# One fused attention and MLP kernel on one core: q loaded in 1 KB runs with token groups outermost, 64x64 state tiles, a new load order and a list-scheduled TensorE order

## The chip, the cores and the metric

The kernel runs on one core of one Trainium2 chip. The metric is device time in microseconds (us), from the start of the program to its end, so smaller is better. The kernel before takes 224.86 us (median of 3 runs, 224.59 to 225.25). Every later comparison ran both kernels in turn on one chip. On this core most executions of one kernel agree within about 1%; a run that is over 1.5% above the fastest of its kernel counts as slow and is left out of ratios. The medians quoted include every run; where a slow run is among them the text says so.

## The reference

Linear attention with decay over 4 batches, 8 heads, 768 tokens and head size 64, then an MLP with a "snake" activation on the 3072 tokens, 512 features and 2048 hidden features:

```python
# attention, block by block (per head, lam is the decay)
intra = einsum('bhic,bhjc->bhij', qb, kb) * Dmask          # lam ** (i - j), lower triangle
out   = einsum('bhij,bhjd->bhid', intra, vb) + einsum('bhid,bhde->bhie', qb * lam_pow, kv_state)
kv_state = lam_block * kv_state + einsum('bhsd,bhse->bhde', kb_dec, vb)
# MLP on x = (tokens, heads * 64)
h = x @ w_in
s = sin(alpha * h)
g = h + s * s / (alpha + 1e-9)
return g @ w_out                                           # (3072, 512) float32
```

## The kernel before

A step is 128 tokens of one batch, all 8 heads; there are 24 steps, and six in a row share one state. A chunk is four steps, 512 tokens, and the MLP works on chunks. The decay is folded into q and k ("scaling"): q is multiplied by lam to the power n, k by lam to the power -n, so that the mask is only triangular. Per step TensorE does:

- *transposes* of q and k (from step 13 on a DMA transposes them instead),
- *scores*, k·q, eight matmuls of 128 columns (`att_S`),
- *inter*, the state times q (`att_O`, first half), *intra*, v times the masked scores (second half),
- *state*, k times v, added to the state in PSUM.

Between the attention groups stand the *big matmuls*, 512 columns each: 64 a chunk for w_in (stage A, `grp_A`) and 64 a chunk for w_out (stage B, `grp_B`). A0 is stage A of chunk 0, and so on. After A0 and B0 come A1 with the attention of chunk 2, and then a steady state in which B of one chunk and A of the next alternate, with two chunks' worth of lead in the attention.

```python
def load_one(nme, s):                       # q, k and v alike: 256-byte runs (64 float32)
    ...
    a = src[b, :, n * BL:(n + 1) * BL, :].rearrange("h p d -> p h d")
    rec_load(lambda e: e.dma_start(dst[r][:, :, :], a), ...)

def prep(s, fast=False, soft=()):           # scaling of k and q, on GpSimd or on VectorE
    ...
    dve_k, dve_q = s == 3, fast and s != 2
    done = rec("DVE" if dve_k else "POOL", lambda e: e.tensor_tensor(k2[c], k32[r][:, :, :], Lk_b, ALU.mult), ...)
    rec("DVE" if dve_q else "POOL", lambda e: e.tensor_tensor(q2[c], q32[r][:, :, :], Lq_b, ALU.mult), ...)

def att_S(s):                               # scores
    for jp in range(HP):                    # head pairs
        for h in range(2):
            rows = slice(64 * h, 64 * h + 64)
            e.matmul(A_ps[:, 4 * h + jp, :], qkT[j][rows, 4 + jp, :], qkT[j][rows, jp, :])
    ...                                     # VectorE: S_m = A_ps * mask

def att_O(s, bank=None):
    if has_state:                           # inter: block-diagonal 128x128 state, four matmuls
        for jp in range(HP):
            e.matmul(dst[:, jp, :], Zs[(s - 1) % 2][:, jp, :], qkT[jq][:, jp, :], ...)
    for jp in range(HP):                    # intra
        for h in range(2):
            e.matmul(dst[64 * h:64 * h + 64, jp, :], v2[c][:, 2 * jp + h, :], S_m[j][:, 4 * h + jp, :], ...)
    ...
    rec("ACT", lambda e: e.copy(xT[x][:, :, col:col + 128], dst), ...)      # x copy
    ...                                     # then the state matmuls, and two copies of the state into Zs
```

A recorder collects these operations with their dependencies, and a scheduling function lays them out on the engines with assumed durations. For TensorE it keeps the order of the program; the other engines take whichever ready operation is first. In stage B0 the attention groups of steps 4 to 7 are placed by hand between the 16 w_out groups:

```python
T_B, S_B, O_B = (2, 6, 10, 12), (3, 7, 11, 13), (5, 10, 12, 15)
...
for m4 in range(4):
    for s4 in range(4):
        op = grp_B(0, s4, m4, banks[s4])
        i = 4 * m4 + s4
        if i in T_B: att_T(4 + T_B.index(i))
        if i in S_B: att_S(...); prep_next(...)
        if i in O_B: att_O(...); prep_v_next(...)
```

GpSimd squares most of the sines (`u`), scales most of q and k and issues the loads of the weights; ScalarE does the sines (`t`) and most copies out of PSUM; VectorE does the masks, the sums (`gT`), the squares that are left, and some of the scaling.

## Time and profile before

224.86 us; the profiled execution spans 222.9 us. Where each stage starts, by the first big matmul of it in the timeline:

| | A0 | B0 | A1 | B1 | end |
|---|---|---|---|---|---|
| start, us | 23.04 | 37.77 | 60.50 | 81.48 | 222.9 |
| length, us | 14.73 | 22.73 | 20.98 | 141.4 | |

The page cuts the span in 40 equal slices of 5.6 us; a digit is the busy share in tenths, for PEclk the clock granted to TensorE:

```profile
PE   6865999998999999999999999999999999999995
...
PEclk9999799999999999999999999999999999999999
DMA  6999999999999999999999533063031011100212
```

TensorE is busy all the time after the start. The DMA engines are busy up to slice 22. The clock is full but for slice 5, where the first big matmuls start.

The groups of the attention matmuls and of two ScalarE copies (line, engine, operation, tile, inputs, shapes, count, then busy us in all and mean ns of one, then idle time before them and its cause):

```profile
L448 PE MATMUL A_ps<-qkT 64*128 64x128 bf16 x192 | 9.5, 218 | 1.1 <-DVE qkT L439 1.0
L469 PE MATMUL A_ps<-qkT,Zs 128*128 128x128 bf16 x68 | 6.6, 219 | 0.2 <-DVE S_m L453 0.2
```

```profile
L496 ACT CAST Zs<-Z_ps 64x256 bf16<-64x256 f32 x40 | 14.6, 366 | 1.6 <-DVE qkT L439 1.0
L482 ACT CAST xT<-A_ps 128x512 bf16<-128x512 f32 x20 | 11.7, 586 | 15.1 <-PE A_ps L473 15.0
```

L448 is scores, L469 inter (four 128x128 matmuls), L482 the x copy, L496 the state copy, of which each step has two. Matmul ends overlap, so the time of a group is better read from starts. In the timeline of the steady state (start, us from first start to last end, engine, line and so on):

```profile
124.64 0.40 PE L448 MATMUL A_ps<-qkT 64*128 64x128 bf16 x8
124.97 1.04 PE L509 MATMUL m_ps<-xT,w 128*128 128x512 bf16 x4
...
128.44 0.39 PE L469 MATMUL A_ps<-qkT,Zs 128*128 128x128 bf16 x4
128.75 0.41 PE L473 MATMUL A_ps<-S_m,v_2 128*64 128x128 bf16 x8
```

Eight scores take 124.97 - 124.64 = 0.33 us, inter 128.75 - 128.44 = 0.31 us. From one scores group to the next it is 8.14 us in steady state (I call this the period), of which 32 big matmuls are 6.9.

The load queue, q1, with packets, megabytes and the time of its packets as a share of 16 engines' span:

```profile
q1 hardware_dynamic: 86640, 21.90, 52.3%
```

And one detail that mattered later: at the end of A0, VectorE and GpSimd, in their own timelines:

```profile
39.07 1.21 DVE L407 TENSOR_TENSOR qk_4<-q_4,Lq 128x512 bf16<-128x512 f32 x1
```

### The profile page before, as it was taken

The page shows a single profiled execution, that of the slowest core. Times are in us where ns is not written, and L with a number is a line of the kernel's source. Part 1 is how long each engine was busy: PE and PEld are TensorE (multiplying, and loading weights), DVE is VectorE, ACT ScalarE, POOL GpSimd, SP SyncE. Part 2 cuts the span into 40 slices and gives each one's busy share as a digit, 9 for nine tenths or more (in the row PEclk, how much of TensorE's full clock was granted, in tenths as well). Part 3 has the DMA queues.
Part 4 walks back from the last instruction along what each step waited for, and adds up shares of the span by engine and source line. Part 5 has one row for each costly group of instructions (what it writes and reads, how often), then busy time and mean ns, then how long its engine had stood idle before and what let it go on. Part 6 is the DMA issues. An engine that isn't in the chain of part 4 may idle for free.

```text
span 222.9 us, 3787 instructions
## 1 busy us (share of the span) xinstructions
PE 209.1 (94%) x1513; PEld 102.9 (46%) x1539; DVE 119.7 (54%) x160; ACT 121.8 (55%) x216; POOL 133.9 (60%) x141
## 2 busy tenths in 40 slices
PE   6865999998999999999999999999999999999995
PEld 2443344454555444445445444445445444444454
DVE  2674189736868994645545454553553535544300
ACT  3354688131498976575575556566556435544220
POOL 3464378661389998668768867867845553355000
PEclk9999799999999999999999999999999999999999
DMA  6999999999999999999999533063031011100212
GB/s 133 219 216 201 195 196 220 162 229 229 268 284 221 222 201 236 215 244 180 245 221 201 141 94 94 1 96 96 19 79 47 0 50 47 47 37 10 79 65 94
DMA packets 94513, 32.50 MB, mean 146 GB/s; under 512 B 87184, under 2 KB 91552, under 8 KB 94496
## 3 DMA queue, kind: packets, MB, share of 16 engines
q1 hardware_dynamic: 86640, 21.90, 52.3%
q0 software_dynamic: 4224, 4.19, 11.4%
q10 hardware_dynamic: 3632, 6.17, 7.6%
q8 instruction: 12, 0.20, 0.4%
q14 instruction: 5, 0.04, 0.1%
HBM read 27.28 MB, written 6.29 MB: 151 GB/s over the span
## 4 chain that ended last, share of the span: by engine, by line
PE 81%; DVE 6%; SPq 5%; DMA 3%; ACT 2%; issue 2%; POOL 0%
PE m_ps L509 34%; PE m_ps L537 34%; SPq L335 5%; PE A_ps L473 3%; PE A_ps L448 3%; DMA v_3<-in_v_dram 3%; DVE gT L527 2%; PE A_ps L469 2%; PE m_ps L562 2%; DVE S_m L453 1%; PE A_ps L434 1%; PE Z_ps L488 1%; PE A_ps L436 1%; DVE u_3 L525 1%; DVE qkT L439 1%
## 5 line engine op out<-in xcount | busy, mean ns | idle before, releaser
L509 PE MATMUL m_ps<-xT,w 128*128 128x512 bf16 x366 | 92.5, 382 | 2.3 <-issue 1.7
L537 PE MATMUL m_ps<-w,gT 128*128 128x512 bf16 x362 | 90.6, 379 | 0.6 <-issue 0.3
L537 PEld LDWEIGHTS m_ps<-w,gT 128*128 128x128 bf16 x368 | 34.9, 98 | 42.2 <-ACT osb L549 1.3
L509 PEld LDWEIGHTS m_ps<-xT,w 128*128 128x128 bf16 x384 | 35.1, 98 | 41.3 <-issue 1.5
L453 DVE TENSOR_TENSOR S_m<-A_ps,mask 128x1024 bf16<-128x1024 f32 x24 | 29.4, 1223 | 9.7 <-PE A_ps L448 9.7
L525 POOL TENSOR_TENSOR u_0<-t_0 128x512 bf16<-128x512 bf16 x16 | 16.6, 1038 | 13.9 <-ACT t_0 L513 13.9
L527 DVE SCALAR_TENSOR_TENSOR gT<-u_3,r_sb,m_ps 128x512 bf16<-128x512 bf16 x16 | 11.9, 744 | 15.0 <-POOL u_3 L525 14.9
L482 ACT CAST xT<-A_ps 128x512 bf16<-128x512 f32 x20 | 11.7, 586 | 15.1 <-PE A_ps L473 15.0
L525 POOL TENSOR_TENSOR u_2<-t_2 128x512 bf16<-128x512 bf16 x15 | 15.6, 1037 | 7.3 <-ACT t_2 L513 7.3
L525 POOL TENSOR_TENSOR u_4<-t_4 128x512 bf16<-128x512 bf16 x15 | 15.6, 1039 | 7.0 <-ACT t_4 L513 7.0
L527 DVE SCALAR_TENSOR_TENSOR gT<-u_5,r_sb,m_ps 128x512 bf16<-128x512 bf16 x16 | 11.9, 746 | 14.1 <-POOL u_5 L525 14.1
L527 DVE SCALAR_TENSOR_TENSOR gT<-u_1,r_sb,m_ps 128x512 bf16<-128x512 bf16 x16 | 11.9, 744 | 14.0 <-POOL u_1 L525 14.0
L527 DVE SCALAR_TENSOR_TENSOR gT<-u_0,r_sb,m_ps 128x512 bf16<-128x512 bf16 x16 | 11.9, 743 | 11.5 <-POOL u_0 L525 11.5
L549 ACT COPY osb<-m_ps 128x512 f32<-128x512 f32 x19 | 11.1, 585 | 11.7 <-PE m_ps L537 11.7
L525 POOL TENSOR_TENSOR u_5<-t_5 128x512 bf16<-128x512 bf16 x12 | 12.5, 1039 | 7.9 <-ACT t_5 L513 7.8
L513 ACT ACTIVATE t_0<-m_ps,alpha_sb 128x512 bf16<-128x512 f32 x16 | 11.0, 685 | 10.8 <-PE m_ps L509 10.8
L513 ACT ACTIVATE t_2<-m_ps,alpha_sb 128x512 bf16<-128x512 f32 x16 | 11.0, 687 | 10.7 <-PE m_ps L509 10.5
L525 POOL TENSOR_TENSOR u_3<-t_3 128x512 bf16<-128x512 bf16 x12 | 12.5, 1038 | 7.3 <-ACT t_3 L513 7.2
L513 ACT ACTIVATE t_4<-m_ps,alpha_sb 128x512 bf16<-128x512 f32 x16 | 11.0, 687 | 10.7 <-PE m_ps L509 10.7
L525 POOL TENSOR_TENSOR u_1<-t_1 128x512 bf16<-128x512 bf16 x12 | 12.4, 1037 | 7.2 <-ACT t_1 L513 7.2
L496 ACT CAST Zs<-Z_ps 64x256 bf16<-64x256 f32 x40 | 14.6, 366 | 1.6 <-DVE qkT L439 1.0
L513 ACT ACTIVATE t_3<-m_ps,alpha_sb 128x512 bf16<-128x512 f32 x16 | 11.0, 687 | 8.0 <-PE m_ps L509 8.0
(190 smaller groups left out, 238.0 us busy)
## 6 DMA issues: line engine op xcount, KB each, us to landing
out_dram<-osb ACTq DMA_DIRECT2D x23, 256.0 KB, 2.7
w<-in_moe_w_in_dram POOLq DMA_DIRECT2D x4, 512.0 KB, 11.5
w<-in_moe_w_out_dram POOLq DMA_DIRECT2D x4, 512.0 KB, 12.8
k_0<-in_k_dram SPq DMA_DIRECT2D x4, 256.0 KB, 5.1
q_0<-in_q_dram SPq DMA_DIRECT2D x4, 256.0 KB, 4.8
k_1<-in_k_dram SPq DMA_DIRECT2D x4, 256.0 KB, 5.2
q_1<-in_q_dram SPq DMA_DIRECT2D x4, 256.0 KB, 5.6
v_0<-in_v_dram SPq DMA_DIRECT2D x4, 256.0 KB, 4.9
```

The costliest lines, as they stand in the source:

```text
L335: rec_load(lambda e: e.dma_start(dst[r][:, :, :], a), [f"{nme}32.{r}"], f"{nme}{r}", 321000, [gate[s]] if s in gate else [])
L448: last = e.matmul(A_ps[:, 4 * h + jp, :], qkT[j][rows, 4 + jp, :], qkT[j][rows, jp, :])
L453: rec("DVE", lambda e: e.tensor_tensor(S_m[j2][:, :, :], A_ps[:, :, :], mask_b, ALU.mult), 1.25, reads=["S0", "S1", "mask"], writes=[f"S_m ...
L473: last = e.matmul(dst[64 * h:64 * h + 64, jp, :], v2[c][:, 2 * jp + h, :], S_m[j][:, 4 * h + jp, :], start=(not has_state and jp == 0), st ...
L482: rec("ACT", lambda e: e.copy(xT[x][:, :, col:col + 128], dst), 0.6, reads=[key], writes=[f"x.{x}.{s % 4}"], prio=-1)
L496: rec("ACT", lambda e, rows=rows, cols=cols: e.copy(Zs[j][rows, :, cols], Z_ps[rows, :, :]), 0.4, reads=["Z"], writes=[f"Zs.{j}"])
L509: last = e.matmul(m_ps[i][:, :], w1[:, kc, 128 * m:128 * (m + 1)], xT[x][:, kc, :], start=(kc == 0), stop=(kc == NKC - 1))
L513: rec("ACT", lambda e: e.activation(t16[tt][:, :], m_ps[i][:, :], ACTF.Sin, scale=alpha_sb[:, m:m + 1]), 0.65, reads=[f"m.{i}", "alpha"], ...
L525: return e.tensor_tensor(u16[tt][:, :], t16[tt][:, :], t16[tt][:, :], ALU.mult)
L527: rec("DVE", lambda e: e.scalar_tensor_tensor(out=gT[g][:, m, :], in0=u16[tt][:, :], scalar=r_sb[:, m:m + 1], in1=m_ps[i][:, :], op0=ALU.m ...
L537: last = e.matmul(m_ps[bank][:, :], gT[g][:, m, 128 * s4:128 * (s4 + 1)], w2[:, m, :], start=(m == 0), stop=(m == NM - 1))
L549: rec("ACT", lambda e: e.copy(osb[o][:, :], m_ps[bank][:, :]), 0.6, reads=[f"m.{bank}"], writes=[f"o.{o}"])
```

## The change

The intent was to shorten the start and the first B stage, and to take work off TensorE:

1. q comes in runs of four tokens, 1 KB. Partition p holds tokens 4i to 4i+3 of one head pair, with p = 4i + g: token groups outermost, head pairs g innermost. So the columns of the transposed q of one head pair lie 4 elements (8 bytes) apart, and attention's output comes out in the order (t, i). The x copy writes it back in token order, with a step of 8 bytes.
2. k and q of steps 0 to 3 are loaded first and v last; transposes, scores and masks of these steps are done before v is there.
3. The state is kept as eight 64x64 tiles, not as four block-diagonal 128x128 ones; one state copy instead of two. The state matmuls go before inter and intra.
4. TensorE's order is found by list scheduling in a window of 40 groups, with a slack of 0.2 us; the hand placement in B0 goes. Some work changes its engine and the loads of w_out are issued at other points.

The core of the diff (cuts marked):

```diff
@@ schedule
-                    op = pe_seq[pe_at]                 # TensorE in the order of the program
...
+                if e == "PE":
+                    ready = [o for o in ready if pe_rank[o] < pe_at + window]
...
+                op = min((o for o in ready if max(free[e], ready_at[o]) <= t0 + (slack if e == "PE" else 0) + 1e-9),
+                         key=lambda o: (o.prio, o.idx))
@@ load_one
+            if nme == "q":
+                for h in range(2):
+                    a = src[b, h::2, n * BL:(n + 1) * BL, :].rearrange("g (p t) d -> p g (t d)", t=4)
+                    rec_load(lambda e, h=h, a=a: e.dma_start(
+                        q32[r][:, h, :, :].rearrange("p t d -> p (t d)"), a), ...)
@@ attention
+        def q_cols(j, rows, jp):
+            return qkT[j][rows, 0:4, jp::4]
...
-                        last = e.matmul(A_ps[:, 4 * h + jp, :], qkT[j][rows, 4 + jp, :], qkT[j][rows, jp, :])
+                        last = e.matmul(A_ps[:, 4 * h + jp, :].rearrange("p (t i) -> p t i", t=4),
+                                        qkT[j][rows, 4 + jp, :], q_cols(j, rows, jp))
...
-                        e.matmul(dst[:, jp, :], Zs[(s - 1) % 2][:, jp, :], qkT[jq][:, jp, :],
-                                 start=(jp == 0), stop=False, skip_group_check=True)
+                        for h in range(2):
+                            rows = slice(64 * h, 64 * h + 64)
+                            e.matmul(dst[rows, jp, :].rearrange("p (t i) -> p t i", t=4), Zs[(s - 1) % 2][rows, jp, :],
+                                     q_cols(jq, rows, jp), start=(jp == 0), stop=False, skip_group_check=True)
...
-            rec("ACT", lambda e: e.copy(xT[x][:, :, col:col + 128], dst), 0.6, reads=[key],
+            copy(eng, xT[x][:, :, col:col + 128].rearrange("p a (i t) -> p a t i", t=4),
+                 dst.rearrange("p a (t i) -> p a t i", t=4), 0.75, reads=[key], writes=[f"x.{x}.{s % 4}"], prio=-1)
...
-                for h in range(2):
-                    rows, cols = slice(64 * h, 64 * h + 64), slice(64 * h, 64 * h + 64)
-                    rec("ACT", lambda e, rows=rows, cols=cols: e.copy(
-                        Zs[j][rows, :, cols], Z_ps[rows, :, :]), 0.4, reads=["Z"], writes=[f"Zs.{j}"])
+                rec("ACT", lambda e: e.copy(Zs[s % 2][:, :, :], Z_ps[:, :, :]), 0.4, reads=["Z"],
+                    writes=[f"Zs.{s % 2}"], prio=-2)
@@ program
-        for what in ("k0", "q0", "k1", "q1", "v0", "k2", "q2", "v1", "k3", "q3", "v2", "v3"):
+        for what in ("k0", "q0", "k1", "q1", "k2", "q2", "k3", "q3", "v0", "v1", "v2", "v3"):
...
+        w2_block(0, soft=[op])
...
         for m in range(NM):
             op = grp_A(0, m)
-            if m in W2_A:
-                w_block(6 + W2_A.index(m), after=[op])
-        prep_next(4, fast=True, soft=[op])
+            if m == 12:
+                w2_block(1, after=[op])
+        prep_next(4, soft=[op], eng_q="DVE")
...
+        att_T(4, bank=spare)
+        for s in range(4, 8):
+            prep(s + 1, soft=[op], eng_q="DVE" if s == 6 else "POOL")
+            prep_v_next(s + 1, [op])
+            att_S(s)
+            if s < 7:
+                att_T(s + 1, bank=spare)
+            att_O(s)
```

## The prediction

> **What bounds the kernel now.** TensorE is busy 209.1 of 222.9 us (busy table); 34% + 34% of the chain that ended last are the big matmuls. The windows show four stages:
> - 0 to 23.04 us: bound by loads. The DMA engines are saturated from 2.5 us; each 256 KB load lands 1.18 us after the last. The chain is SyncE issues, v_3 landing at 19.1, its cast, x and state copies, the last attention matmuls, the first big matmul at 23.04. The first w_in block arrives only then too (0.5 us wait). The clock has fallen: the first big matmuls are 0.43 us apart, later 0.216.
> - First B stage with attention 4 to 7, to 60.5: TensorE idle 1.8 of 22.7 us, on qkT, masks, q scaling, loads.
> - To 81.5: idle 0.5, GpSimd 93% busy.
> - To 206: no gaps. One attention step takes 8.14 us: 32 big matmuls (6.9), 1.2 of attention (scores 0.33 + 0.09 on entry, inter 0.31, intra 0.25, state 0.23). Only less TensorE work helps.
>
> **What the change does.**
> 1. q in 1 KB runs. The load queue's 86,640 packets, mostly 256 B, took 52.3% of 16 engines' span, 21.5 ns each; output packets (1.7 KB) 75 ns. The Trainium skill, "DMA: Bandwidth & Descriptors", Specifications, puts line rate at 512 B and more; the trace agrees (12 against 23 GB/s per engine). Estimate: a q load falls from 1.18 to 0.75 us, 1.7 us over four, on the chain.
> 2. k and q first, v last: transposes, scores, masks of steps 0 to 3 are done before v arrives; after v_3 remain cast, O and x copy (2.3 us, against 3.9 now). The first w_in half block competes with v_2 and v_3 and takes back about 1 us. Big matmuls start at 20.6; gain of 1 and 2 together 2.4 us.
> 3. List scheduling fills idle time in the B stage and after: 1.2 us.
> 4. 64x64 state tiles: eight small matmuls in pairs instead of four full ones. From the intra group's rate 0.31 falls to 0.23, less one more tile switch: 0.07 x 17 = 1.2 us.
> 5. One transposed step fewer on TensorE: 0.45 us.
> 6. Off the path: one state copy instead of two on ScalarE (0.76 to 0.4), strided x copies (0.59 to 0.75).
>
> Scores and inter now read q with a step of 8 bytes. The Trainium skill, "SBUF — State Buffer", Door 1, says that accesses hitting a 16-byte line twice keep full rate, which this does. No trace shows it yet; I assume no loss.
>
> Sum 5.3 us: predicted **219.5 us**, 8 in 10 between **216.8 and 222.0**. Faster by over 2% **0.62**, within 2% **0.35**, slower **0.03**.
>
> **What would show each step.** (1) The load queue falls to about 68,000 packets, its share by 6 to 8 points. (2) First big matmul at 20 to 21.2 us, v_3 landing near 18.3. (3) From the first B matmul to the second A stage 21.3 us instead of 22.7. (4) Steady period 8.05 to 8.10 us; inter 0.23. (5) Twelve qkT copies from PSUM, twelve DMA transposes.
>
> **What would make it wrong.** Strided q halving the matmul rate (+0.3 us per step, about +7 us). w_in delaying v_3, or late for chunk 0, so that the start gains nothing. A low clock in chunk 0 (up to 1.7 us; 0.85 is lost now), or none. The new TensorE order, planned with other durations, waiting behind a late operand. GpSimd bounding the 60 to 81 us stage, so that time won before is waited for again.

## More of the kernel before

```profile
38.69 1.04 POOL L525 TENSOR_TENSOR u_2<-t_2 128x512 bf16<-128x512 bf16 x1
39.67 0.81 POOL L396 DMA_DIRECT2D w<-in_moe_w_out_dram  x1
```

VectorE's scaling of q for step 4, normally 0.68 us, took 1.21 and ended at 40.28, that is 0.55 us after GpSimd's square had ended at 39.73.

## The result, and the profile after

The changed kernel is correct and takes **242.41 us** (median of 4 runs, 240.91 to 242.83) against 225.03 for the kernel before on the same chip: 7.6% slower, outside the predicted range. A ratio in this document is the mean time of one kernel's fast runs over the mean time of the other's in the same rounds, so it is not quite the ratio of the medians quoted; here it is 1.0763, 95% interval 1.0713 to 1.0813.

| | A0 | B0 | A1 | B1 | end |
|---|---|---|---|---|---|
| start before, us | 23.04 | 37.77 | 60.50 | 81.48 | 222.9 |
| start after, us | 22.51 | 41.25 | 69.43 | 90.74 | 240.4 |
| stage longer by, us (the stage that begins there) | 4.01 | 5.45 | 0.33 | 8.24 | |

The start is 0.53 us shorter, the rest 18.0 longer. The slices of the page:

```profile
PE   6977991999979999999999999999999999999995
...
PEclk9999998599999999999999999999999999999999
DMA  4999999989899107989698750330230111011122
```

There is a new hole in slice 7, where TensorE's share falls to 1, and a lower clock in that slice (8) and above all in the next (5). The waits of TensorE show it as a single one, and the timeline shows what the clock does (the last bracket is the idle time before the row and what ended it):

```profile
41.25 3.59 PE L578 MATMUL m_ps<-w,gT 128*128 128x512 bf16 x8 [4.84 <-DVE gT L568]
44.78 0.42 PE L500 MATMUL Z_ps<-v_4,qk_4 128*64 128x64 bf16 x8
```

Eight big matmuls take about 3.5 us (44.78 - 41.25) here; in the kernel before twelve take 2.65 in the same place. The wait is for `gT`, made by VectorE. VectorE and GpSimd at that time:

```profile
33.90 0.73 DVE L568 SCALAR_TENSOR_TENSOR gT<-u_4,r_sb,m_ps 128x512 bf16<-128x512 bf16 x1
34.55 5.98 DVE L432 TENSOR_TENSOR qk_4<-q_4,Lq 128x512 bf16<-128x512 f32 x1
40.46 0.73 DVE L568 SCALAR_TENSOR_TENSOR gT<-u_5,r_sb,m_ps 128x512 bf16<-128x512 bf16 x1
```

```profile
34.12 0.81 POOL L421 DMA_DIRECT2D w<-in_moe_w_out_dram  x1 [1.19 <-PE m_ps L550]
34.95 1.06 POOL L566 TENSOR_TENSOR u_5<-t_5 128x512 bf16<-128x512 bf16 x1
35.96 1.05 POOL L566 TENSOR_TENSOR u_0<-t_0 128x512 bf16<-128x512 bf16 x1
36.95 1.04 POOL L566 TENSOR_TENSOR u_2<-t_2 128x512 bf16<-128x512 bf16 x1
37.95 1.04 POOL L430 TENSOR_TENSOR qk_4<-k_4,Lk 128x512 bf16<-128x512 f32 x1
38.95 1.03 POOL L430 TENSOR_TENSOR qk_0<-k_5,Lk 128x512 bf16<-128x512 f32 x1
```

The scaling of q for step 4 takes 5.98 us instead of 0.68 to 1.21. GpSimd had waited 1.19 us for TensorE at the issue of a w_out load (the one that the change moved behind the thirteenth tile), then worked off five operations without a pause until 39.98. VectorE's operation ended at 40.53, 0.55 us later.

The attention groups and the copies:

```profile
L480 PE MATMUL A_ps<-qkT 64*128 64x128 bf16 x192 | 14.9, 286 | 2.1 <-ACT qkT L443 1.5 <-ACT xT L443 0.4
L522 PE MATMUL A_ps<-qkT,Zs 64*64 64x128 bf16 x136 | 10.7, 288 | 0.4 <-DVE S_m L485 0.4
```

```profile
L443 ACT CAST xT<-A_ps 128x512 bf16<-128x512 f32 x20 | 26.1, 1305 | 16.5 <-PE A_ps L526 16.5
...
L506 ACT CAST Zs<-Z_ps 128x256 bf16<-128x256 f32 x20 | 7.8, 390 | 8.8 <-PE Z_ps L500 8.8
```

Scores (L480) went from 218 to 286 ns a matmul, inter (L522) has twice the matmuls at 288 ns, the x copy (L443) takes 1305 ns instead of 586, and the state copy (L506) is one of 390 ns instead of two of 366. In the steady state:

```profile
120.34 0.62 PE L480 MATMUL A_ps<-qkT 64*128 64x128 bf16 x8
120.89 1.04 PE L550 MATMUL m_ps<-xT,w 128*128 128x512 bf16 x4
...
124.45 0.32 PE L500 MATMUL Z_ps<-v_0,qk_0 128*64 128x64 bf16 x8
124.70 0.63 PE L522 MATMUL A_ps<-qkT,Zs 64*64 64x128 bf16 x8
125.25 0.41 PE L526 MATMUL A_ps<-S_m,v_0 128*64 128x128 bf16 x8
```

Scores take 0.55 us (120.89 - 120.34), inter 0.55 (125.25 - 124.70). The period is 8.82 us instead of 8.14. The load queue did what was predicted, 17,000 packets fewer. Its share is 10.7 points smaller, of a longer span: 41.6% of 240.4 us is 100.0 us, against 116.6 before, which is 7.4 points of the old span:

```profile
q1 hardware_dynamic: 69648, 22.16, 41.6%
```

And at the start, ScalarE before the first big matmul (the last load of the start, v_3, landed at 16.80 us, against 19.10 in the kernel before, where its cast began at once):

```profile
16.95 1.33 ACT L443 CAST xT<-m_ps 128x512 bf16<-128x512 f32 x1
...
18.37 0.63 ACT L443 CAST v_3<-v_3 128x512 bf16<-128x512 f32 x1
```

The cast of v_3 waits 1.57 us behind an x copy. Two more x copies, 19.80 to 22.23 us, come before the first big matmul at 22.51.

### The profile page after: what moved, and what is told of

The parts are those of the page before. It is cut to its first block, busy times and chain, and to the rows that moved or that the text cites. A ratio compares the mean times of both kernels' runs of the same rounds, so it can differ in the third digit from the quotient of the medians.

```text
span 240.4 us, 3953 instructions
## 1 busy us (share of the span) xinstructions
PE 222.9 (93%) x1587; PEld 106.8 (44%) x1613; DVE 123.3 (51%) x158; ACT 129.6 (54%) x198; POOL 137.8 (57%) x147
## 3 DMA queue, kind: packets, MB, share of 16 engines
q1 hardware_dynamic: 69648, 22.16, 41.6%
## 4 chain that ended last, share of the span: by engine, by line
PE 85%; DVE 6%; ACT 5%; issue 2%; POOL 1%; POOLq 0%
PE m_ps L578 33%; PE m_ps L550 31%; PE A_ps L480 5%; PE A_ps L522 4%; PE A_ps L526 3%; PE m_ps L620 3%; ACT xT L443 3%; DVE qk_4 L432 2%; PE Z_ps L500 2%; DVE gT L568 1%; PE m_ps L603 1%; ACT qkT L443 1%; PE m_ps L463 1%; PE m_ps L465 1%; DVE S_m L485 0%
## 5 line engine op out<-in xcount | busy, mean ns | idle before, releaser
L578 PE MATMUL m_ps<-w,gT 128*128 128x512 bf16 x362 | 93.5, 388 | 5.4 <-DVE gT L568 4.8
L550 PEld LDWEIGHTS m_ps<-xT,w 128*128 128x128 bf16 x384 | 34.6, 98 | 44.0 <-issue 2.9
L443 ACT CAST xT<-A_ps 128x512 bf16<-128x512 f32 x20 | 26.1, 1305 | 16.5 <-PE A_ps L526 16.5
L568 DVE SCALAR_TENSOR_TENSOR gT<-u_3,r_sb,m_ps 128x512 bf16<-128x512 bf16 x16 | 11.9, 744 | 16.8 <-POOL u_3 L566 16.8
L568 DVE SCALAR_TENSOR_TENSOR gT<-u_1,r_sb,m_ps 128x512 bf16<-128x512 bf16 x16 | 11.9, 745 | 16.1 <-POOL u_1 L566 15.6
L568 DVE SCALAR_TENSOR_TENSOR gT<-u_5,r_sb,m_ps 128x512 bf16<-128x512 bf16 x16 | 11.9, 745 | 14.3 <-POOL u_5 L566 14.3
L590 ACT COPY osb<-m_ps 128x512 f32<-128x512 f32 x21 | 12.4, 591 | 11.6 <-PE m_ps L578 11.6
L554 ACT ACTIVATE t_4<-m_ps,alpha_sb 128x512 bf16<-128x512 f32 x16 | 11.0, 688 | 11.8 <-PE m_ps L550 11.8
L568 DVE SCALAR_TENSOR_TENSOR gT<-u_0,r_sb,m_ps 128x512 bf16<-128x512 bf16 x16 | 11.9, 742 | 10.5 <-POOL u_0 L566 10.5
L554 ACT ACTIVATE t_2<-m_ps,alpha_sb 128x512 bf16<-128x512 f32 x16 | 11.0, 688 | 11.3 <-PE m_ps L550 11.3
L480 PE MATMUL A_ps<-qkT 64*128 64x128 bf16 x192 | 14.9, 286 | 2.1 <-ACT qkT L443 1.5
L554 ACT ACTIVATE t_0<-m_ps,alpha_sb 128x512 bf16<-128x512 f32 x16 | 11.0, 687 | 10.4 <-PE m_ps L550 10.4
L568 DVE SCALAR_TENSOR_TENSOR gT<-u_2,r_sb,m_ps 128x512 bf16<-128x512 bf16 x16 | 11.9, 742 | 8.2 <-POOL u_2 L566 8.2
```

The source lines that it names most:

```text
L443: rec("ACT", lambda e: e.copy(dst, src), dur, **kw)
L480: last = e.matmul(A_ps[:, 4 * h + jp, :].rearrange("p (t i) -> p t i", t=4), qkT[j][rows, 4 + jp, :], q_cols(j, rows, jp))
L550: last = e.matmul(m_ps[i][:, :], w1[:, kc, 128 * m:128 * (m + 1)], xT[x][:, kc, :], start=(kc == 0), stop=(kc == NKC - 1))
L554: rec("ACT", lambda e: e.activation(t16[tt][:, :], m_ps[i][:, :], ACTF.Sin, scale=alpha_sb[:, m:m + 1]), 0.65, reads=[f"m.{i}", "alpha"], ...
L568: rec("DVE", lambda e: e.scalar_tensor_tensor(out=gT[g][:, m, :], in0=u16[tt][:, :], scalar=r_sb[:, m:m + 1], in1=m_ps[i][:, :], op0=ALU.m ...
L578: last = e.matmul(m_ps[bank][:, :], gT[g][:, m, 128 * s4:128 * (s4 + 1)], w2[:, m, :], start=(m == 0), stop=(m == NM - 1))
```

## The experiments

Eighteen kernels ran. The time of the kernel before that is quoted with each is its median on the same chip. "Wrong" means that the outputs are wrong and only the time is of interest; in such kernels the decay factors are set so that the sines' arguments stay small. The theories that the expectations speak of are these. Theory A: TensorE reads q more slowly with a step of 8 bytes. Theory B, the x copies cost the time. Theory C: GpSimd's backlog holds up VectorE's operations with both inputs in SBUF. Theory E, which came later: the list-scheduled order is itself a loss. The rivals are named in the expectations.

### First call: one cause removed at a time

**a1_contig_q**: read q contiguously (wrong).

```diff
-            return qkT[j][rows, 0:4, jp::4]
+            return qkT[j][rows, jp, :].rearrange("p (t i) -> p t i", t=4)
```

> Changed kernel, but TensorE reads q contiguously in the scores and the inter product (wrong data on purpose; decays set to 1 so that values stay in range). Theory A (a step of 8 bytes in the moving operand halves its rate): eight score matmuls fall from 0.55 to 0.33 us, eight inter matmuls from 0.55 to about 0.25-0.31, the steady period from 8.82 to about 8.3, the time by 8 to 10 us, to about 233. Rival B (the cost is the 64x64 tiles and switching between tile shapes): the groups stay at 0.55 and the time moves by less than 2 us.

Measured: 234.59 us (before: 224.80), ratio 1.0388. One of the four runs behind this median is slow; by the ratios, which use fast runs alone (1.0763 against 1.0388), the gain on the changed kernel is 8.4 us. Scores are back at 0.33 us, inter is 0.34. The profiled run itself fell in a slow state, so I take no stage times from it, and the period only because it is the same, 8.38 us, over four steps in a row, twice (the fast run e2 has it too). Theory A holds; the wait of 4.9 us at the first w_out matmul stayed, so something else is left.

**a2_contig_x**: write x without a step (wrong: its columns are in another order).

```diff
-            copy(eng, xT[x][:, :, col:col + 128].rearrange("p a (i t) -> p a t i", t=4),
-                 dst.rearrange("p a (t i) -> p a t i", t=4), 0.75, ...)
+            copy(eng, xT[x][:, :, col:col + 128], dst, 0.75, ...)
```

> Changed kernel, but x is written in the order in which it leaves PSUM, contiguously (rows of the result permuted, so wrong on purpose). Theory: the x copy on ScalarE falls from 1.31 to 0.59 us; first big matmul 1.3 us earlier than 22.51, and 0.7 us less wait at the second A stage; total gain 1.5 to 2.5 us (240 us). Rival: x copies are off the path everywhere but at the start, and what the start gains is waited for again at the stall of VectorE near 35 us: gain under 0.7 us.

Measured: 242.28 us, ratio 1.0762, as slow as the changed kernel, though the x copy is back at 0.586 us. The period stays at 8.82 us, so the x copies cost nothing in the steady state. The first big matmul started at 22.61 and B0 only at 44.18, but for the start this is no clean test: in the profiled run the clock was low from 17.5 to 27.8 us, 5.2 us into A0. What the copies cost there is taken up under the prediction's start, below.

**a3_q4_pool**: scale q of step 4 on GpSimd, so that the 6 us operation is not there (correct).

```diff
-        prep_next(4, soft=[op], eng_q="DVE")
+        prep_next(4, soft=[op])
```

> Changed kernel, but the q scaling of step 4 runs on GpSimd instead of VectorE (result stays right). Theory C (that VectorE instruction, 5.98 us instead of 0.69, is held off by GpSimd instructions running back to back): no VectorE scaling over 2 us, the TensorE wait of 4.84 us before the first B matmul falls under 1 us, and the clock does not fall after it; gain 6 to 7.5 us, to about 235.5. Rival D (the new access pattern, or its data arriving late, makes it long): the GpSimd scaling becomes several us long instead of 1.05, and the gain is under 2 us.

Measured: 243.16 us, ratio 1.0812: no gain, and a wait of 5.66 us in the same place. The timeline of VectorE shows why:

```profile
36.87 5.82 DVE L566 TENSOR_TENSOR u<-t 128x512 bf16<-128x512 bf16 x1 [0.81 <-ACT t L554]
```

Another operation, the square of the fourteenth tile, normally 0.41 to 0.58 us, takes 5.82 us now, while GpSimd works without a pause from 36.38 to 42.40. So it is not the scaling operation that is slow: here whichever VectorE operation with both inputs in SBUF comes next, waits. The `gT` operations, which take one input from PSUM, do not: in the kernel before 41 of the 96 lie wholly beside a GpSimd operation, and their median is 0.74 us, against 0.75 for those that lie beside none.

**a4_all**: the three edits at once (wrong).

> The three edits before together (wrong on purpose). If the three causes add up and are all: 242.4 - 9.5 - 2 - 6.5, about 224.5 us. If the rest of the change gives the 5.3 us predicted, about 219.5; if it costs by itself (tile switches, other order), 226 or more.

Measured: 233.16 us, ratio 1.0342, only 1.0 us better than the read alone (by the ratios), with the first big matmul at 21.54 us and the wait of 5.66 us still there. My sum for this run, which counted on the wait going, failed with a3.

### Second call: the wait, the read in the other direction, a mended read

**a6_w2_early**: issue the second w_out block early, as the kernel before does (correct).

```diff
-        w2_block(0, soft=[op])
+        op = w2_block(0, soft=[op])
+        w2_block(1, soft=[op])
...
-            if m == 12:
-                w2_block(1, after=[op])
```

> The changed kernel with one edit: the second w_out block is issued by GpSimd right after the first, as the kernel before did, not after the thirteenth tile of chunk 0. The result is correct. Theory C (the issue of that block waits for TensorE on GpSimd, puts GpSimd behind, and the squares that it then runs without a pause hold up VectorE's next operation with both inputs in SBUF for five to six microseconds): the GpSimd backlog goes, no VectorE operation of the A0 stage takes over 1.5 us, the wait at the first B matmul falls from 4.84 us to under 1 us, the clock does not fall in the B stage, and the kernel gains 6 to 7.5 us, to about 235 us. Rival D (the load of w_out or of step 4 itself holds VectorE, or the stall is only the slowest of several late operands): the wait stays above 3 us or turns into another one of the same size and the time stays within 1.5 us of 242.4.

Measured: 242.19 us, ratio 1.075. The expected gain is not there. The wait at the start of B0 is gone (A0 takes 13.66 us, better than before's 14.73), but B0 takes 29.7 us instead of 28.2 and A1 22.7 instead of 21.3. Four new waits stand in it, from the timeline of TensorE:

```profile
43.05 0.40 PE L463 MATMUL m_ps<-ident,qk 128*128 128x128 bf16 x4 [1.96 <-DVE qk L432]
...
62.48 0.62 PE L480 MATMUL A_ps<-qkT 64*128 64x128 bf16 x8 [1.44 <-ACT xT L443]
64.42 0.63 PE L522 MATMUL A_ps<-qkT,Zs 64*64 64x128 bf16 x8 [1.32 <-DVE S_m L485]
...
67.19 2.81 PE L550 MATMUL m_ps<-xT,w 128*128 128x512 bf16 x7 [1.24 <-ACT v L443]
```

The first is theory C again, a little later: the scaling of q for step 4 started at 40.17, GpSimd was busy until 42.44, and it ended at 43.00. The others come at the end of B0: the list order has used up the w_out groups and there is nothing left to fill the waits of step 7 with. One edit moved the whole plan, so this run does not test the issue alone.

**a7_no2port**: leave the issue where it is, but give VectorE no operation with both inputs in SBUF in that stretch (correct).

```diff
-            if (c == 0 and m in (3, 8, 13)) or ...      # squares on VectorE
+            if (c == 0 and m in (3, 8)) or ...
-            elif (c == 0 and m in (5, 10, 15)) or ...   # squares on ScalarE
+            elif (c == 0 and m in (5, 10, 13, 15)) or ...
-        prep_next(4, soft=[op], eng_q="DVE")
+        prep_next(4, soft=[op])
```

> The changed kernel with two edits: step 4's q scaling moves from VectorE to GpSimd and the square of the fourteenth tile of chunk 0 from VectorE to ScalarE, so that VectorE has no operation with both inputs in SBUF while GpSimd works off its backlog. The result is correct, and the w_out issue stays where the change put it. Theory C: the 5 us VectorE operation disappears although GpSimd is as far behind as before, the wait at the first B matmul falls below 2 us (GpSimd's own backlog may still delay a square), gain 4 to 7 us. Rival (GpSimd's backlog itself delays the last squares, VectorE's long operation is only a sign of it): the wait stays above 4 us and the time at 242 us.

Measured: 236.68 us, ratio 1.0498: 5.7 us gained by moving two operations to other engines, although GpSimd has one operation more. The wait falls from 4.84 to 0.52 us and B0 runs at full clock. Theory C holds, its rival (GpSimd's own backlog is the delay) does not.

**b1_stride**: the kernel before, with q read with a step of 8 bytes (wrong).

```diff
-                        last = e.matmul(A_ps[:, 4 * h + jp, :], qkT[j][rows, 4 + jp, :], qkT[j][rows, jp, :])
+                        last = e.matmul(A_ps[:, 4 * h + jp, :].rearrange("p (t i) -> p t i", t=4), qkT[j][rows, 4 + jp, :],
+                                        qkT[j][rows, 0:4, jp::4])      # and the same in inter
```

> The kernel before with one edit, wrong on purpose: scores and inter matmuls read q with a step of 8 bytes, nothing else changes (decay factors set to 1 to keep arguments small). Theory A (a step of 8 bytes halves the rate at which TensorE takes its moving operand): scores 0.33 becomes 0.55 us, the inter matmuls 0.31 become 0.55 us, the steady period 8.14 becomes 8.55 to 8.65 us, and the kernel takes 233 to 236 us. Rival (the slower scores came from the 3-dimensional output, from tile shapes, or from a lower clock after the stall): scores stay at 0.33 and the time within 1 us of 224.8.

Measured: 232.69 us (before: 225.32), ratio 1.0322, so 7.4 us lost by this alone. Scores 0.55, inter 0.55 although it has still four 128x128 matmuls, period 8.60. Taking the step away gave 8.4 us, putting it in costs 7.4: the read is 7 to 8.5 us of the 17.4.

**c2_gmajor**: the changed kernel with q's partitions ordered with the head pair outermost, so that TensorE reads runs of 64 bytes, and the early w_out block (correct).

```diff
-                for h in range(2):
-                    a = src[b, h::2, ...].rearrange("g (p t) d -> p g (t d)", t=4)       # two loads of 128 KB
+                for g in range(4):
+                    a = src[b, 2 * g:2 * g + 2, ...].rearrange("h (p t) d -> p h (t d)", t=4)   # four of 64 KB
...
-            return qkT[j][rows, 0:4, jp::4]
+            return qkT[j][rows, 0:4, 32 * jp:32 * jp + 32]
```

> The changed kernel with two edits, correct by design: the 1 KB runs of q stay, but the q tile's partitions are ordered with the head pair outermost, so that the transposed q has each head pair's 32 tokens of a group in consecutive columns and TensorE reads runs of 64 bytes instead of single elements with a step of 8; and the w_out block is issued early as in the kernel before. Theory A and C together: scores 0.33 us, inter 0.34, no wait over 1 us at the first B matmul, and the gain of both, 7.8 us (as the contiguous q run showed) and 6 to 7 us, so 227 to 229 us, still not below the kernel before because the period keeps about 0.1 to 0.15 us of extra tile switches. Rival for the read (only fully contiguous 256-byte runs are fast): scores stay near 0.5 us and the time at 235 us.

Measured: 240.82 us, ratio 1.0679. The reads are mended (scores 222 ns a matmul, 0.33 us a group), but the first big matmul starts at 27.07 us, over 4 us later. The loads, four of 64 KB on 32 partitions each in place of two of 128 KB, explain only part of it: v_3 lands at 18.44 us instead of 16.80. Its cast then waits for ScalarE until 23.35, in a start in which the clock is low from 17.6 to 31.3 us; how these share the rest is not shown. And late waits like those of a6 come with the early w_out block (2.0 us in two waits, 1.8 and 1.1, at the end of B0 and the start of A1). The gain of the read was spent again.

### Third call: tiles, order, and the first attempt at a sum

**b2_tiles**: the kernel before with 64x64 state tiles and one state copy (correct), 5 rounds.

```diff
-                        e.matmul(dst[:, jp, :], Zs[(s - 1) % 2][:, jp, :], qkT[jq][:, jp, :], ...)
+                        for h in range(2):
+                            rows = slice(64 * h, 64 * h + 64)
+                            e.matmul(dst[rows, jp, :], Zs[(s - 1) % 2][rows, jp, :], qkT[jq][rows, jp, :], ...)
```

> The kernel before with one edit, correct: the state is kept as 64x64 tiles with one state copy per step, and the four 128x128 inter matmuls become eight 64x64 ones; q stays contiguous. My prediction: inter 0.31 becomes 0.23 us, the steady period 8.14 becomes 8.07 us, 223.6 us in all. Rival (eight 64x64 matmuls take 0.34 us, as the run with contiguous q showed, and entering or leaving such tiles costs about 0.1 us): period 8.15 to 8.25 us and 225 to 226.5 us.

Measured: 225.18 us (before: 224.79), ratio 1.0016, interval 0.9966 to 1.0066. No gain; inter takes 0.34 us, not 0.23, and the period is 8.26 us instead of 8.14. The Trainium skill, "TensorEngine Tiling (Array Packing)", Key Properties, says that a change of tiling mode drains TensorE. The trace agrees in kind: the eight 64x64 matmuls take 0.03 us more than the four they replace, and the other 0.09 us lies in front of them: from the fourth-last big matmul to the first inter matmul it is 0.96 us, against 0.87 before.

**b3_sched**: the kernel before with the list scheduler (correct). The edit is the whole scheduling function, of which the first hunk of the change's diff shows the core; it also plans a deeper load queue.

> The kernel before with one edit, correct: the scheduling function of the changed kernel, which may reorder TensorE's groups within a window of 40, in place of the fixed TensorE order; the loads, q's layout and the tiles stay. My prediction: 1.2 us faster, 223.6 us. Theory E (the plan's durations are off, so the order that it makes runs out of w_out matmuls to fill waits in the first B stage, as the late waits of 1.2 to 1.4 us there showed in the run with the early w_out block): the first B stage and the A stage after it get longer by 2 us or more in sum and the kernel takes 226.5 to 229 us. Rival: the list order is harmless, and the lost time of the changed kernel comes from its own operations alone: within 0.7 us of the kernel before.

Measured: 227.88 us, 3.1 us more than before, ratio 1.0113, interval 1.0068 to 1.0158, where I had predicted 1.2 us less. A0 and B0 are 0.9 and 1.5 us longer. B0 contains new waits (1.1 us for a w_out block, 1.1 us for a mask); in A0 it is a lower clock at the start, low until 26.95 us against 24.65 before: at half speed from the first big matmul on that is 1.8 us lost instead of 0.8 (an estimate). The period stays at 8.14. So about 2 of the 3.1 us are the order's own, in the stages with waits, where the planned durations decide; in the steady state it costs nothing. Why the clock stays low for longer is not shown.

**d1_hand**: the changed kernel with TensorE in program order and the hand placement in B0 (correct).

```diff
-    def schedule(self, ..., window=40, slack=0.2):
+    def schedule(self, ..., window=1, slack=0.2):
...                                     # B0: the T_B, S_B, O_B placement of the kernel before
```

> The changed kernel with one part undone, correct: TensorE's groups stay in the order of the program (window of one), and in the first B stage the attention groups are put between the w_out groups at the places where the kernel before had them; loads, layout of q, tiles and GpSimd's order of issues stay as changed. Theory E: the first B stage falls from 28.2 to 25 us or less, of which about 23 is the kernel before's and 2 the slower reads, and the time falls from 242 to 236 to 238 us. Rival (the order of the groups matters little; the long VectorE operation and the cold clock after it are the whole loss there): the wait of 4 to 6 us at the first B matmul stays, the stage stays at 27 to 28 us and the time at 240 to 242.

Measured: 245.20 us, ratio 1.0894, slower than the changed kernel. The program order of the changed kernel was not made to be run as it stands: the first big matmul starts at 26.33 us, since the window also served the start. The wait at the first w_out matmul is 3.94 us, B0 28.1. So the rival's reading holds for B0: the long VectorE operation and the clock after it are the larger loss there, the order the smaller.

**d3_gm_hand_w2**: mended reads in two loads, hand placement, early w_out block (correct).

```diff
-                    a = src[b, h::2, ...].rearrange("g (p t) d -> p g (t d)", t=4)
+                    a = src[b, h::2, ...].rearrange("g (p t) d -> g p (t d)", t=4)   # the order of partitions, and of the dimensions of the DMA
```

> The changed kernel with three edits, correct by design: q's partitions ordered with the head pair outermost (runs of 1 KB stay, two loads a step as in the changed kernel, TensorE reads runs of 64 bytes), TensorE in the hand-placed order, and the early w_out block. What stays of the change: 1 KB runs, k and q first and v last, 64x64 tiles, strided x copy. All three theories together: scores 0.33 us, first big matmul at 22 to 23 us (the four-load form cost 4 us at the start, this should not), no wait over 1.2 us in the first B stage, which takes 22.5 to 24 us, and 225 to 228 us in all. If the time stays above 232 us, a cause is missing.

Measured: 260.92 us, ratio 1.1596, the slowest of all. A cause was indeed missing, and it was one of my own edit: with the four head pairs as the outermost dimension of the load, the loads are slow. The first slices of the page, DMA and GB/s, against those of the changed kernel (4, 9, 9, 9 and 120, 273, 217, 225):

```profile
DMA  2458999698766658999889987912033101111122
GB/s 61 133 146 172 212 197 196 138 178 182 199 189 190 134 139 172 141 154 213 188 153 177 218 154 155 168 49 47 36 84 82 41 3 41 41 43 41 41 81 81
```

The first big matmul starts at 33.9 us. The changed kernel has the same bytes in the same 1 KB runs with the 32 token groups outermost. The DMA records of the two traces show how they differ. Over the first 16 us of d3 never more than 6 packets of q are in flight at once, mostly 4, as many as the load's outermost dimension has rows; in the changed kernel it is up to 22. Between 3 and 12 us one such packet takes 49 ns on average in d3 and 59 in the changed kernel, so it is not the single packet that is slow. The load is spread less widely; that the outermost dimension is what decides it is the likely reading, since no run varies it alone. The run does show that "token groups outermost" was not a free choice: the layout that is good for TensorE's read is bad for the load.

### Fourth call: the sum, the backlog in the kernel before, the step

**e1_start**: the changed kernel without its costly parts: q loaded and read as before, x written without a step, early w_out block, hand placement from the first big matmul on (a window of 40 only for the first 26 groups), state matmuls last again (correct), 5 rounds.

> The changed kernel without the parts that were found to cost time, correct: q loaded and read as before (256-byte runs, contiguous reads), x copied contiguously, the early w_out block, and TensorE in the hand-placed order from the first big matmul on. What stays of the change: k and q loads first and v last with the matching order of the first four steps, the split first w_in block, 64x64 tiles with one state copy, one transposed step fewer on TensorE. If all losses are known: first big matmul at 22 to 23 us, a first B stage of 22 to 23.5 us, a period of 8.13 to 8.2, and 222.5 to 225.5 us, so the same as before within 0.7%. If a part that stays costs time by itself: over 227 us.

Measured: 229.13 us (before: 224.77), ratio 1.0193; the expectation failed by about 4 us. The first big matmul starts at 22.71 us, the periods are those of 64x64 tiles, 8.26, but B0 takes 27.2 us. The long VectorE operation is there again:

```profile
40.63 2.80 DVE L407 TENSOR_TENSOR qk<-q,Lq 128x512 bf16<-128x512 f32 x1
```

```profile
40.00 0.81 POOL L397 DMA_DIRECT2D w<-in_moe_w_out_dram  x1
40.82 1.06 POOL L405 TENSOR_TENSOR qk<-k,Lk 128x512 bf16<-128x512 f32 x1
41.83 1.05 POOL L407 TENSOR_TENSOR qk<-q,Lq 128x512 bf16<-128x512 f32 x1
```

GpSimd's run ends at 42.88, VectorE's operation at 43.43, 0.55 us later; TensorE waits 2.89 us for it. So in my own supposedly cleaned kernel the early w_out block did not prevent the collision. In the kernel before the two engines just happened to be timed so that VectorE waited for one operation only.

**e2_closure**: the changed kernel with contiguous reads, no VectorE operation with both inputs in SBUF at the end of chunk 0, and the hand placement from the first big matmul on (wrong).

> The changed kernel with three parts taken out at once, wrong on purpose: q is read contiguously (decay factors 1), no VectorE operation with both inputs in SBUF at the end of chunk 0, and TensorE in the hand-placed order from the first big matmul on. What stays: the 1 KB loads, strided x copies, tiles, late w_out block. If the causes add (7.6 for the read, 5.8 for VectorE's long operation, 2 to 2.6 for the order): 242.4 - 15.5 = 227 us, between 225.5 and 229. If they are the same loss seen twice, or one is missing: above 231 us.

Measured: 228.43 us (one of the four runs is slow; the fast ones have a median of 228.34), ratio 1.0214. Expected were 227, between 225.5 and 229. The causes add to within 1.5 us. B1 starts at 81.69 us, 0.21 after the kernel before; what is left comes after that: the period is 8.38 us instead of 8.14, of which 0.12 is the tiles (b2) and 0.12 more, by difference, the state matmuls placed before inter.

**b4_w2_late**: the kernel before with its second w_out block issued after the thirteenth tile of chunk 0 (correct).

```diff
-                for j in range(1, 6):
+                for j in range(1, 5):
                     w_block(j, soft=[done])
...
+            if m == 12:
+                w_block(5, after=[op])
```

> The kernel before with one edit, correct: its second w_out block is issued by GpSimd after the thirteenth tile of chunk 0, as the changed kernel does; TensorE's order is unchanged. Theory C: GpSimd waits for TensorE at the issue, gets behind, runs squares and scalings without a pause, and VectorE's next operation with two inputs in SBUF (q scaling of step 4) takes 3 to 6 us instead of 1.2; a wait of 2 to 5 us appears at the first B matmuls and the kernel takes 227 to 231 us. Rival (the backlog needs the changed kernel's other differences): no wait over 1 us and within 1 us of the kernel before.

Measured: 229.44 us, ratio 1.0219: 4.7 us lost by moving one issue, with TensorE's order unchanged. VectorE, then GpSimd:

```profile
34.89 4.99 DVE L407 TENSOR_TENSOR qk<-q,Lq 128x512 bf16<-128x512 f32 x1
```

```profile
34.47 0.81 POOL L396 DMA_DIRECT2D w<-in_moe_w_out_dram  x1 [1.19 <-PE m_ps L509]
35.29 2.05 POOL L525 TENSOR_TENSOR u<-t 128x512 bf16<-128x512 bf16 x2
37.29 1.04 POOL L405 TENSOR_TENSOR qk<-k,Lk 128x512 bf16<-128x512 f32 x1
38.29 1.03 POOL L525 TENSOR_TENSOR u<-t 128x512 bf16<-128x512 bf16 x1
```

The same picture as in the changed kernel: a wait of 1.19 us at the issue, then a run until 39.32, and VectorE ends at 39.88. TensorE waits 3.8 us.

Such a long wait is not what always happens when the two engines meet. In the kernel before, at 75 us, a square on VectorE waits for one operation of GpSimd only, and the next one of GpSimd, which follows without a pause, is lengthened from 1.04 to 1.22 us:

```profile
75.36 1.23 DVE L525 TENSOR_TENSOR u_3<-t_3 128x512 bf16<-128x512 bf16 x1 [0.16 <-ACT t_3 L513]
```

```profile
76.27 1.22 POOL L405 TENSOR_TENSOR qk_2<-k_0,Lk 128x512 bf16<-128x512 f32 x1
```

In the twenty traces GpSimd gave way like this 33 times. VectorE waited through a whole run of operations, for 2 us or more, nine times, and in all nine GpSimd's run began right behind the issue of a w_out load (above, VectorE's operation begins at 34.89 us, within that issue). So a run without a pause alone does not explain the long wait; what the issue adds to it is not shown.

**b5_step4**: the kernel before, q read with a step of 4 bytes (wrong on purpose), one look.

> The kernel before with one edit, wrong on purpose: scores and inter read q with a step of 4 bytes (every second element). If a 16-byte line has to be hit at least twice for full rate, as the Trainium skill's SBUF page says, scores stay at 0.33 us as they should have with 8 bytes. If any step above one element costs the same: 0.55 us, as with 8 bytes. If the cost follows the bytes passed over: about 0.40 to 0.45 us.

Measured: 224.87 us in one run, so its state is unknown (before: 224.77). Scores 219 ns a matmul, period 8.15. A step of 4 bytes costs nothing.

### The last two runs

**f1_512**: the kernel before with q in runs of two tokens, 512 bytes, so laid out that TensorE reads 64 elements at a time without a step (correct), 5 rounds. Odd steps copy x the other way round: they write without a step and read PSUM with one.

```diff
+            if nme == "q":
+                for g in range(2):                                    # head quads, 64 partitions each
+                    a = src[b, 4 * g:4 * g + 4, n * BL:(n + 1) * BL, :].rearrange("w (p t) d -> p w (t d)", t=2)
...
+            return qkT[j][rows, u:4:2, 64 * g:64 * g + 64]
...
+            order = "p a i t" if s % 2 else "p a t i"
+            ... e.copy(xT[...].rearrange("p a (i t) -> " + order, t=2), dst.rearrange("p a (t i) -> " + order, t=2))
```

> The kernel before with q alone changed, correct by design: q in runs of two tokens (512 bytes), two loads of 128 KB a step with 64 partitions each, head quads outermost in the partitions, so that TensorE reads q in runs of 64 elements with no step inside; x written back in token order with a step of 4 bytes in even steps, and read from PSUM with a step instead in odd ones. TensorE's order, 128x128 tiles, load order and GpSimd's order stay as in the kernel before. If longer runs help (packets 86,640 to about 74,000; v_3 landing 0.4 to 0.8 us earlier) and the reads are free: scores 0.33, period 8.14, first big matmul at 22 to 22.8 us and 223.5 to 225 us. If the x copies take 1.3 us as with a step of 8 bytes, the start gains nothing: 224.5 to 226. If half-width loads cost rate: first big matmul after 24 us and over 226.

Measured: 225.90 us (before: 225.10), ratio 1.0055, interval 1.0012 to 1.0098. Scores 0.33 us, period 8.14: the read is mended and the steady state is that of the kernel before. But nothing is gained:

```profile
q1 hardware_dynamic: 74736, 21.90, 52.9%
```

There are 11,900 packets fewer than before in the same share of time, and v_3's cast starts at 19.54 us against 19.12. Between 3 and 12 us a 512-byte packet takes 41 ns on average, a 256-byte packet of the kernel before 22: nothing gained per byte. A 1 KB packet takes 59 ns in the changed kernel, whose q loads fill 128 partitions, and 82 in c2, with 32 each, so the narrow loads may be the reason. The x copies take 0.73 us where they write with a step of 4 bytes, and 0.59 where they write without a step and read PSUM with one of 256 bytes. No version beats the kernel before.

**b6_step16**: the kernel before, its moving operand read with a step of 16 bytes (wrong on purpose), one look.

> The kernel before with one edit, wrong on purpose: scores and inter read their moving operand with a step of 16 bytes (every eighth element, over the q and the k columns of the same tile). If the read costs in proportion to the bytes passed over beyond 4 bytes an element: scores 1.0 to 1.1 us, inter 1.0 us, period about 9.5 us, 245 us or more. If any step of 8 bytes or more costs one fixed factor: 0.55 us as with 8 bytes, period 8.6, about 232 us. [...]

Measured: 250.76 us in one run, state unknown (before: 225.00). Scores take 1.00 us, the period is 9.50. With the other runs on the kernel before:

| step of the moving operand, bytes | 2 | 4 | 8 | 16 |
|---|---|---|---|---|
| scores, eight matmuls, us | 0.33 | 0.33 | 0.55 | 1.00 |
| period, us | 8.14 | 8.15 | 8.60 | 9.50 |

From 8 to 16 bytes the scores grow by 0.45 us, from 4 to 8 by 0.22: proportional to the bytes passed over beyond 4 an element, so the first case of the expectation.

## Why the prediction was wrong, point by point

The prediction said 219.5 us; it was 242.41. What the change cost, by the runs in which one part was done or undone alone:

| cause | undone in the changed kernel | done alone in the kernel before |
|---|---|---|
| q read with a step of 8 bytes | -8.4 us (a1, by the ratios) | +7.4 us (b1) |
| VectorE held up by GpSimd, and the low clock after it | -5.7 us (a7) | +4.7 us (b4) |
| list-scheduled order | no clean run (d1 is 2.8 us slower, its start 3.8 us later) | +3.1 us (b3; 2.5 by the ratio; about 1.0 of it low clock in A0) |
| 64x64 tiles | | +0.4 us (b2; by the ratio -0.8 to +1.5) |
| state matmuls before inter | about +1.3 us: 0.12 us a period over 11 periods, by difference of periods | |

Where nothing else is said these are differences of medians; the kernel before took 224.8 to 225.3 us on all chips. The sum is 16.9 us with the right-hand column and 18.9 with the left where it has a number; measured were 17.4, with 0.5 gained at the start. The run with the three largest undone at once (e2) came out at 228.4 against an expected 227. The losses are thus found to within about 1.5 us.

- **The step that failed most: "Scores and inter now read q with a step of 8 bytes. ... I assume no loss."** I took this from the Trainium skill, "SBUF — State Buffer", Door 1, which says that two hits on a 16-byte line suffice for full bandwidth. A step of 8 bytes has two hits a line, and scores went from 0.33 to 0.55 us. The prediction itself named this as the first thing that could make it wrong and gave its size, "+0.3 us per step, about +7 us"; measured were 0.46 us a period and 7.4 to 8.4 us. I saw the risk and gave it no weight in the sum: that, more than the statement on the page, was the mistake.
- **"List scheduling fills idle time in the B stage and after: 1.2 us."** Wrong in sign: +3.1 us alone (b3). And its neighbour in the change, the later issue of w_out, cost another 5. My list of what could go wrong has "the new TensorE order, planned with other durations, waiting behind a late operand" and "a low clock", but not the chain that happened: GpSimd waits for TensorE at an issue, gets behind, runs without a pause; VectorE's next operation with both inputs in SBUF waits for the whole run; `gT` waits behind it in VectorE's order; TensorE idles 4.84 us; its clock falls. The Trainium skill, "SBUF — State Buffer", the section on SBUF's two separate sides, describes a lock between VectorE and GpSimd, and I had not used it. The trace agrees with the page that there is an exclusion, and that `gT` with one input from PSUM escapes it. It differs in the length: the page gives the lock for one instruction, but here VectorE waited through five (after), four (b4) and six (a3) of GpSimd's instructions in a row. Elsewhere in the same traces it waited for one, as on the page (see b4).
- **"64x64 state tiles: inter 0.31 falls to 0.23."** Inter took 0.34 (a1, b2), and the period grew by 0.12 us. Eight small matmuls went no faster than the four large ones, and the tile changes came on top. I had allowed "one more tile switch" and still taken a gain.
- **"Big matmuls start at 20.6; gain of 1 and 2 together 2.4 us."** They start at 22.51, so 0.53 us gained. The loads did better than predicted: v_3 landed at 16.80 us (predicted 18.3, before 19.10; 18.20 in e1, with the new order but 256-byte runs). That its cast begins at 18.37, close to the predicted landing, is chance. The step that failed is the path behind the landing: I counted 2.3 us from v_3 to the first big matmul, and it took 5.7. I had the strided x copies at 0.75 us and "off the path"; they take 1.31 to 1.33 us, and at the start ScalarE is the path: one copy holds up v_3's cast until 18.37, and two more stand one behind the other from 19.80 to 22.23. From the first of these two to the first big matmul it is 2.6 to 2.8 us where copies write with the step (after, a3, a6, a7, e2), and 1.4 (a4) and 1.9 (a2) where they write without, so the step costs about 1 us there. Kernels with the start of the changed one began their big matmuls between 22.04 (a3) and 23.82 us (a6, a7); in the two latest the clock was low from 18.3 to 21.7 us.
- **"One transposed step fewer on TensorE" and the copies off the path** were too small to be seen. The state copy was 0.39 us as predicted (0.4), and the transposes moved to the DMA as counted. The x copies, twice as long as predicted, cost no time in the steady state (a2), as predicted.
- **Right:** the bound (TensorE, then and now), the packets (69,648 against "about 68,000") and their share (7.4 points of the old span, predicted 6 to 8; 10.7 as the page gives it).
- The clock: the stall of 4.84 us was followed by slices at 0.8 and 0.5 of the clock, and the w_out matmuls in them started about 0.44 us apart instead of 0.216. The Trainium skill, "TensorE: Matmul & The Clock Gate", Part 1, describes this: an idle window of about 3.4 us halves the clock. This wait agrees: TensorE idles from 36.41 to 41.25 us and the record has the clock at half from 40.28 to 47.11. Not all do: in e1 it fell at 44.71 us, after a wait of 2.89 us that had ended at 43.58, and in a6 at 66.06, with waits of 1.44 and 1.32 us before it. So a wait can cost more than its own time: the eight matmuls lose 1.7 us (44.78 - 41.25 = 3.53 us for what takes 1.8 at full clock), and up to 47.11 about 2.9 are lost in all (an estimate, half of 5.86 us at half clock). The gain of a7, 5.7 us with 4.3 us of wait removed, contains it.

What stays open: how much of B0's remaining excess is the order and how much the cold clock in d1; why VectorE gets in after one of GpSimd's operations in most places and after the whole run behind a w_out issue; whether the outermost dimension alone is why the loads in d3 are spread less; and why 512-byte runs in f1 gained nothing while 1 KB runs did (f1 also loads only 64 partitions at a time, so two things were changed).

## What to carry to other kernels

A layout that pleases the DMA moves its cost to every later reader: measure the reader with the new step in the kernel as it is before building the rest, since that is a two-line edit; here a step of 4 bytes was free, 8 bytes took two thirds longer and 16 bytes three times as long. When one engine's operation is suddenly many times its usual length, look at what its neighbour does in that stretch, not at the operation: moving two VectorE operations elsewhere gave back a third of the loss. And a plan made by a scheduler has to be judged by where its waits fall, since an edit that removes one wait can lead the same planner to another of the same size.

## What the Trainium skill lacked or had wrong

- "SBUF — State Buffer", Door 1, gives full bandwidth for two hits on a 16-byte line and a free step of 8 bf16 elements. For TensorE's bf16 moving operand this is wrong: eight scores matmuls take 0.33 us with steps of 2 and 4 bytes, 0.55 with 8, 1.00 with 16 (before, b5, b1, b6). At 16 bytes, 8 bf16 elements, the two statements also disagree with each other, since such a step hits each line once. The rule of two hits also stands in "Advanced Engine Details and Errata", SBUF Cachelines.
- "SBUF — State Buffer", the section on SBUF's two separate sides, gives the exclusion between VectorE and GpSimd for the whole of one instruction. That fits most overlaps here (33 in which GpSimd's next instruction gave way, 1.2 us or more, at 75 us of the kernel before 1.22, instead of 1.04). Missing: in nine, all right behind the issue of a load from GpSimd, VectorE waited through two to six instructions in a row. The scaling of q, 0.68 us when nothing is in its way, ended 0.55 to 0.56 us after the last GpSimd instruction that it waited for in each of six traces, however long it had waited (its length: before 1.21 us, behind one instruction; e1 2.80, a6 2.83, b4 and d1 4.99, after 5.98).
- No page that I read gives the cost of ScalarE's or VectorE's writes with a step. A 128x512 bf16 copy out of PSUM took 0.59 us with no step, 0.73 with 4 bytes, 1.31 with 8 (both engines), and 0.59 with the step of 256 bytes on the PSUM read instead (f1).
- "TensorEngine Tiling (Array Packing)", Key Properties, says that changing the tiling mode drains TensorE, without a price. Here the 64x64 tiles cost 0.12 us a period, and placing the state matmuls before inter another 0.12 (b2, a1, e2).
